# A fourth PSUM bank and another product order for layer 1, and a float64 conversion in 7 operations of 512 columns, in an attention, mixture and feed-forward kernel

## The chip, the cores and the metric

The kernel runs on one core of one Trainium2 chip, as one launch. The metric is the device time of one execution in microseconds (us). Before the change it is 1487.26 us, the median of three runs (1483.48 to 1487.72).

## The reference

Three blocks follow one another. Attention with a band of local keys and a few global keys (2 batches, 8 heads, 768 positions, 64 wide) gives x, 1536 tokens by 512. A mixture of 8 experts and a feed-forward layer then transform it:

```python
P = exp(x @ w_gate - max)
for _ in range(8):
    P /= P.sum(1) + 1e-9;  P /= P.sum(0) + 1e-9;  P *= N / E
for e in range(8):                       # w1[e]: 512 x 1024, w2[e]: 1024 x 512
    out += P[:, e:e+1] * (np.maximum(x @ w1[e], 0) @ w2[e])
h = out @ w_in                           # w_in: 512 x 2048
result = (h * (1 / (1 + np.exp(-1.702 * h)))) @ w_out
```

The last two matrices, w_in and w_out, reach the device as 64-bit floats; the rest is in 32 bits. The device therefore has to make 32-bit floats of w_in and w_out with integer operations before it can use them.

## The kernel before

**Units and steps.** Experts and the feed-forward layer are cut into units of 256 hidden columns: 32 units of the experts (four of each) and 8 of the feed-forward layer. A step works one unit on one of the two batches of 768 tokens, and there are 80 steps, laid out by `plan` (L531). A version is one loading of a unit's weights; most versions serve two steps in a row, one for each batch.

A step is a layer 1 (x by the unit's part of w1, `layer1`, L393) and a layer 2 (hidden values by the unit's part of w2, `layer2`, L472). On TensorE's queue layer 1 of step i stands ahead of layer 2 of step i-1, so layer 2 always reads hidden values that were finished a whole layer 2 earlier. Each full-precision product is made of three products of high and low parts (the names end in h and l, and the split is `split`, L196: ScalarE rounds the high part, GpSimd subtracts for the low part).

**Layer 1** multiplies a 2 by 2 block matrix by a 2 by 2 block matrix with seven products and not eight. Each product is 6 matmuls of 384 columns. The table PRODUCTS (L60) names, for each, the weight sum (A11, S2, ...), the operand sum (B11, T2, ...) and the PSUM bank that it accumulates in: x, y or z. Before, the order is A11 (x), S2 (y), A12 (x), S3 (y), S1 (z), A22 (y), S4 (z). Between the products VectorE forms the sums u2, u3 and p1 from the banks (the helper on L403), and ScalarE copies the first product to p1 (L452). A bank that goes on accumulating must first have been read by the sum that wants its value up to there. So S3 waits for the sum u2 that reads bank y after S2, with one product (A12) between the two; A22 waits for the sum u3 that reads y after S3, with one product (S1) between; S4 waits for the sum that reads z after S1, with one product (A22) between; A12 waits for the copy of x.

`put` (L408) takes a finished block of hidden values: ScalarE applies Relu or Sigmoid, and the rest (the low part, and in the feed-forward layer the multiplication with the sigmoid, L418) is queued behind the next product's matmuls (`late`). In the feed-forward layer each block needs one of two sigmoid buffers (tag "sg").

**Layer 2** has six tiles of 128 tokens, each of 6 matmuls of 512 columns, and each is read out of its PSUM bank by VectorE (L500 scaled by the gate, L498 and L506 without) or, for an expert's first unit, by ScalarE. `psum` (L519) hands out the banks: eight in all, two named s, two named t, one named v and three named m, which hold x, y and z. In phase 2 (attention of the second batch runs between the steps) layer 2 uses the m banks; in phase 3 (gate and normalisation run between the steps) it goes round s, s, t, v; in phase 4 (the rest) it goes round s, s, t, t, and bank v is idle.

**Work in between.** `mixture` (L600) calls `advance` after every product and every layer-2 tile, 13 times a step. Each call adds a rate to a debt, and for each whole number in the debt it emits the next piece of a side task, in the engines' queues at that place. From the step after the gate is ready, the side task is `doubles` (L221) at a rate of 0.55: it converts w_in and w_out and stores them in device memory for the feed-forward units, whose loads (`load_w1` and `load_w2`) come late in the plan. All loads and stores are issued from SyncE's queue.

`doubles` has 64 jobs of 256 columns. A job loads 256 KB (L239), makes nine VectorE operations of 128 by 256 in five pieces (L250 to L263), five with a constant and four with two tensors, all reading SBUF alone, and stores 128 KB (L264).

**Order on the engines.** All queues are in the order in which the program emits work, and VectorE, ScalarE and GpSimd each run theirs in order. Weight splits of the next version (`split_w1`, `split_w2`) are emitted in the second step of a version, one product behind the one that used the same buffer.

## Time and profile before

| what | value |
|---|---|
| median of three runs | 1487.26 us (1483.48 to 1487.72) |
| the profiled execution's own time | 1492.43 us |
| its span, first to last instruction | 1490.4 us |
| mean granted TensorE clock | 0.986 of full speed |
| TensorE matmul, busy | 1422.0 us, 95% |
| VectorE, busy | 1135.6 us, 76% |
| GpSimd, busy | 860.1 us, 58% |
| ScalarE, busy | 644.5 us, 43% |

The profile is of one execution, which took 5.2 us longer than the median of the runs; 2.0 us of its time lie outside the span. A busy engine in it is one with an instruction running; a matmul's end is modelled, so a short idle time of TensorE can be longer than its row says. PE is TensorE, PEld its weight loads, DVE VectorE, ACT ScalarE, POOL GpSimd and SP SyncE.

### The profile page before, as it was taken

What the parts mean: (1) busy time and instruction counts of PE and PEld (TensorE: products, weight loads), DVE (VectorE), ACT (ScalarE), POOL (GpSimd) and SP (SyncE); (2) the same over time, 40 slices, a digit from 0 to 9 for tenths busy, and PEclk for the clock granted to TensorE, in tenths of its full rate; (3) what the DMA queues carried; (4) which work ended last, traced back from release to release, by engine and by line L of the source; (5) the groups of instructions that cost most, each with busy time, mean ns of one, the idle gap of its engine ahead of it and who ended that gap; (6) DMA issues with size and microseconds to landing.
All of it is one profiled execution on the core that took longest, in us unless ns stands there. A gap on an engine that the chain in (4) does not pass through costs nothing.

```text
span 1490.4 us, 21158 instructions
## 1 busy us (share of the span) xinstructions
PE 1422.0 (95%) x7295; PEld 1244.4 (83%) x7295; DVE 1135.6 (76%) x2199; ACT 644.5 (43%) x1511; POOL 860.1 (58%) x1003
## 2 busy tenths in 40 slices
PE   7899998999899999999999999999999988999999
PEld 5567887788888888898888888888888877899897
DVE  7987887467578888888888888788887576555655
ACT  5676767243443333333333333333333456534332
POOL 3645555657674555554555545455555686756652
PEclk9989999999999999999999999999999999999999
DMA  5322210111221222222121212112121111101002
GB/s 147 73 61 60 73 46 29 57 57 57 75 88 62 66 73 72 71 64 68 60 75 64 82 60 72 60 61 75 61 85 47 48 38 34 52 29 43 29 1 85
DMA packets 99348, 91.66 MB, mean 61 GB/s; under 512 B 42912, under 2 KB 76704, under 8 KB 99232
## 3 DMA queue, kind: packets, MB, share of 16 engines
q1 hardware_dynamic: 99232, 90.22, 19.2%
q8 instruction: 60, 0.98, 0.3%
q14 instruction: 56, 0.46, 0.1%
HBM read 78.66 MB, written 11.53 MB: 61 GB/s over the span
## 4 chain that ended last, share of the span: by engine, by line
PE 80%; DVE 13%; issue 3%; ACT 3%; POOL 2%; POOLq 0%; DVEq 0%; ACTq 0%
PE pl L489 41%; PE pl1y L445 14%; PE pl1z L445 10%; PE pl1x L445 8%; PE pv L928 2%; DVE u L403 2%; PE s L850 1%; DVE acc L500 1%; PE pt L887 1%; DVE a L876 1%; POOL w2l L205 1%; DVE acc L285 1%; DVE a L863 1%; DVE al L908 1%; DVE hl L430 1%
## 5 line engine op out<-in xcount | busy, mean ns | idle before, releaser
L489 PE MATMUL pl<-w2h,hl 128*128 128x512 f32 x960 | 300.9, 394 | 6.9 <-DVE acc L500 4.3
L489 PE MATMUL pl<-w2l,hh 128*128 128x512 f32 x960 | 297.2, 391 | 0.0
L489 PE MATMUL pl<-w2h,hh 128*128 128x512 f32 x960 | 297.1, 391 | 0.0
L500 DVE SCALAR_TENSOR_TENSOR acc<-pl,pr,acc 128x512 f32<-128x512 f32 x312 | 230.2, 746 | 74.5 <-PE pl L489 71.9
L205 POOL TENSOR_TENSOR w2l<-r,w2h 128x512 fp32r<-128x512 f32 x100 | 131.5, 1336 | 196.7 <-ACT w2h L199 178.1
L489 PEld LDWEIGHTS pl<-w2l,hh 128*128 128x128 f32 x960 | 180.5, 188 | 39.3
L489 PEld LDWEIGHTS pl<-w2h,hh 128*128 128x128 f32 x960 | 180.4, 188 | 38.8
L489 PEld LDWEIGHTS pl<-w2h,hl 128*128 128x128 f32 x960 | 176.8, 188 | 39.8 <-DVE acc L500 5.7
L425 POOL TENSOR_TENSOR hl<-u,hh 128x384 fp32r<-128x384 f32 x100 | 105.8, 1058 | 135.1 <-ACT hh L422 134.5
L199 ACT ACTIVATE w2h<-r 128x512 fp32r<-128x512 f32 x98 | 56.6, 624 | 207.6 <-PE pl L489 174.3
L403 DVE TENSOR_TENSOR u<-p,pl1y 128x384 f32<-128x384 f32 x160 | 87.8, 549 | 64.7 <-PE pl1y L445 52.5
L452 ACT ACTIVATE p<-pl1x 128x384 f32<-128x384 f32 x80 | 39.2, 490 | 182.2 <-PE pl1x L445 167.6
L403 DVE TENSOR_TENSOR u<-u,pl1z 128x384 f32<-128x384 f32 x160 | 88.1, 551 | 36.2 <-PE pl1z L445 33.7
L421 ACT ACTIVATE u<-u 128x384 f32<-128x384 f32 x100 | 52.1, 521 | 123.6 <-DVE u L403 123.1
L205 POOL TENSOR_TENSOR hl<-sg,hh 128x384 fp32r<-128x384 f32 x64 | 66.0, 1031 | 58.1 <-ACT hh L199 56.7
L205 POOL TENSOR_TENSOR S3l<-s,S3h 128x256 fp32r<-128x256 f32 x50 | 40.5, 810 | 99.4 <-ACT S3h L199 99.2
L192 POOL TENSOR_TENSOR s<-r 128x256 f32<-128x256 f32 x100 | 78.2, 782 | 0.0
L506 DVE TENSOR_TENSOR acc<-pl,acc 128x512 f32<-128x512 f32 x84 | 54.3, 682 | 19.9 <-PE pl L489 19.8
L866 ACT ACTIVATE a<-a,m 128x288 f32<-128x288 f32 (+2 forms) x96 | 48.1, 502 | 43.0 <-DVE m L863 43.0
L445 PE MATMUL pl1y<-T3h,S3l 128*128 128x384 f32 x160 | 44.4, 358 | 23.0 <-DVE u L403 22.9
L427 ACT ACTIVATE hh<-pl1x 128x384 fp32r<-128x384 f32 x64 | 31.4, 491 | 79.5 <-PE pl1x L445 79.4
L205 POOL TENSOR_TENSOR A22l<-r,A22h 128x256 fp32r<-128x256 f32 x50 | 44.0, 880 | 22.6 <-ACT A22h L199 22.3
(259 smaller groups left out, 3489.6 us busy)
## 6 DMA issues: line engine op xcount, KB each, us to landing
r<-in_moe_w_dram SPq DMA_DIRECT2D x82, 512.0 KB, 3.6
r<-d SPq DMA_DIRECT2D x18, 512.0 KB, 3.7
d<-in_moe_w_in_dram SPq DMA_DIRECT2D x32, 256.0 KB, 2.8
d<-cx SPq DMA_DIRECT2D x64, 128.0 KB, 1.7
d<-in_moe_w_out_dram SPq DMA_DIRECT2D x32, 256.0 KB, 3.0
out_dram<-acc SPq DMA_DIRECT2D x12, 256.0 KB, 2.1
k<-in_k_dram SPq DMA_DIRECT2D x28, 96.0 KB, 2.3
q<-in_q_dram SPq DMA_DIRECT2D x28, 96.0 KB, 2.5
```

The source lines that it names most:

```text
L192: nc.gpsimd.tensor_tensor(out=o, in0=x, in1=y, op=op)
L199: nc.scalar.activation(hi, x, AF.Copy)
L205: e.tensor_tensor(out=lo, in0=x, in1=f(hi), op=ALU.subtract)
L403: add = lambda o, x, y: nc.vector.tensor_tensor(out=o, in0=x, in1=y, op=ALU.add)
L421: nc.scalar.activation(c, c, AF.Relu)
L425: nc.gpsimd.tensor_tensor(out=l, in0=c, in1=f(h), op=ALU.subtract)
L445: nc.tensor.matmul(ps, x[:, d, :], y[:, d, :], start=(new and i == 0 and d == 0), stop=(i == 2 and d == 1), skip_group_check=True)
L452: nc.scalar.activation(p1, ps, AF.Copy)
L489: nc.tensor.matmul(ps, x[:, c, ts_], y, start=(i == 0 and c == 0), stop=(i == 2 and c == 1))
L500: nc.vector.scalar_tensor_tensor(out=acc, in0=ps, scalar=self.pr[:, tt, e : e + 1], in1=acc, op0=ALU.mult, op1=ALU.add)
L506: nc.vector.tensor_tensor(out=acc, in0=ps, in1=acc, op=ALU.add)
L866: nc.scalar.activation(s, s, AF.Exp, bias=m, scale=-1.0, accum_out=rs[:, j : j + 1])
```

## The change

From phase 3 on, layer 1 uses another table, WIDE: S3 goes to a bank of its own (w, which is the bank named v), S3 and S1 come before A12, and A22 starts bank y anew and does not go on accumulating in it. The sums change with it: u3 = u2 + w after S3, p1 = u3 + z after S1 (and this block is put there), the block of x is put after A12, and u3 = u3 + y after A22. Every product, sum and put is still made once. In phase 3 layer 2 goes round s, s, t.

`doubles` has 32 jobs of 512 columns with seven operations (three with a constant, four with two tensors) in seven pieces, at a rate of 0.42. Loads are 512 KB each and stores 256 KB; there are 32 of each.

```diff
+    WIDE = [
+        ("A11", "B11", "x"),
+        ("S2", "T2", "y"),
+        ("S3", "T3", "w"),
+        ("S1", "T1", "z"),
+        ("A12", "B21", "x"),
         ("A22", "T4", "y"),
         ("S4", "B22", "z"),
     ]
...
-        C = 256
+        C = 2 * FW
...
-                for _ in range(8):
+                for _ in range(6):
                     yield
...
             nc.vector.tensor_scalar(x, hi, 3, 0x3FFFFFFF, op0=ALU.logical_shift_left, op1=ALU.bitwise_and)
-            nc.vector.tensor_scalar(y, hi, -0x40000000, None, op0=ALU.bitwise_and)
-            yield
-            nc.vector.tensor_tensor(out=x, in0=x, in1=y, op=ALU.bitwise_or)
+            yield
+            nc.vector.scalar_tensor_tensor(out=x, in0=hi, scalar=-0x40000000, in1=x, op0=ALU.bitwise_and, op1=ALU.bitwise_or)
+            yield
+
             nc.vector.tensor_scalar(y, x, -0x800000, None, op0=ALU.bitwise_and)
             yield
-            nc.vector.tensor_scalar(z, lo, 1, None, op0=ALU.logical_shift_right)
-            nc.vector.scalar_tensor_tensor(out=f(z), in0=z, scalar=2.0**-51, in1=f(y), op0=ALU.mult, op1=ALU.mult)
-            yield
-            nc.vector.tensor_tensor(out=f(x), in0=f(x), in1=f(z), op=ALU.add)
+            nc.vector.scalar_tensor_tensor(out=f(y), in0=lo.bitcast(U32), scalar=2.0**-52, in1=f(y), op0=ALU.mult, op1=ALU.mult)
+            yield
+            nc.vector.tensor_tensor(out=f(x), in0=f(x), in1=f(y), op=ALU.add)
+            yield
...
-        for an, bn, k in [self.PRODUCTS[n] for n in (0, 4, 2, 1, 3, 5, 6)] if first else self.PRODUCTS:
+        wide = self.phase >= 3
+        order = self.WIDE if wide else self.PRODUCTS
+
+        for an, bn, k in [order[n] for n in (0, 4, 2, 1, 3, 5, 6)] if first else order:
             ah, al = self.w1[v, an]
             bh, bl = self.xops[b][bn]
-            new = k not in bank
-            if new:
-                bank[k] = self.ps_m.tile([P, HS], F32, tag="m", name=f"pl1{k}_{v}_{b}")
+            new = k not in bank or wide and an == "A22"
+            if k not in bank:
+                p, tag = (self.ps_v, "v") if k == "w" else (self.ps_m, "m")
+                bank[k] = p.tile([P, HS], F32, tag=tag, name=f"pl1{k}_{v}_{b}")
...
+            elif an == "S4":
+                add(u2, u2, ps)
+                put(u2, 0, 1)
+            elif wide:
+                if an == "S3":
+                    add(u3, u2, ps)
+                elif an == "S1":
+                    add(p1, u3, ps)
+                    put(p1, 1, 1)
+                elif an == "A22":
+                    add(u3, u3, ps)
+                    put(u3, 1, 0)
...
-            kinds = {2: "m", 3: "sstv", 4: "sstt"}[self.phase]
+            kinds = {2: "m", 3: "sst", 4: "sstt"}[self.phase]
...
-                    side.append(("doubles", self.doubles(self.cv), 0.55))
+                    side.append(("doubles", self.doubles(self.cv), 0.42))
```

## Rows read from the trace of the kernel before

**Rows 1.** Part 1 of the page: busy time, share of the span, instructions.

```profile
PE 1422.0 (95%) x7295; PEld 1244.4 (83%) x7295; DVE 1135.6 (76%) x2199; ACT 644.5 (43%) x1511; POOL 860.1 (58%) x1003
```

**Rows 2.** Windows: length; PE, PEld, DVE, ACT, POOL busy (instructions); clock, DMA, GB/s.

```profile
387.89:1178.64 790.75, 771.22 (x3823) 688.72 (x3822) 652.89 (x1167) 286.46 (x633) 438.96 (x484) 1.00 0.21 68
1147.59:1178.64 31.05, 31.05 (x157) 28.12 (x156) 15.62 (x24) 11.31 (x25) 17.74 (x21) 1.00 0.12 34
1307.73:1462.90 155.17, 155.17 (x782) 140.52 (x780) 93.41 (x150) 63.13 (x136) 93.29 (x101) 1.00 0.07 24
1400.83:1408.14 7.31, 7.31 (x44) 7.30 (x42) 3.49 (x7) 4.41 (x11) 5.95 (x7) 1.00 0.22 74
```

**Rows 3.** Waits of TensorE from 388 to 1179 us: total, times, longest.

```profile
PE pl1y L445 <- DVE u L403: 18.0, 22, 2.4
```

**Rows 4.** Timeline of VectorE, GpSimd and TensorE in a layer 1 at 709 us.

```profile
709.88 2.59 POOL L205 TENSOR_TENSOR w2l<-r,w2h 128x512 fp32r<-128x512 f32 x2 [5.64 <-ACT w2h L199]
...
711.36 1.40 DVE L257 SCALAR_TENSOR_TENSOR cz<-cz,cy 128x256 f32<-128x256 int32 x1
...
712.00 0.51 PE L445 MATMUL pl1x<-B21h,A12h 128*128 128x384 f32 x2
...
712.68 0.54 DVE L403 TENSOR_TENSOR u<-p,pl1y 128x384 f32<-128x384 f32 x1
...
713.27 0.61 PE L445 MATMUL pl1y<-T3h,S3l 128*128 128x384 f32 x2 [0.76 <-DVE u L403]
```

**Rows 5.** Windows: 2.55 us just after the longest wait of rows 3.

```profile
941.24:943.79 2.55, 2.55 (x9) 2.55 (x9) 0.56 (x1) 0.00 (x0) 0.00 (x0) 0.50 0.47 154
```

**Rows 6.** Waits of TensorE from 250 to 388 us.

```profile
PE pl1y L445 <- DVE u L403: 5.6, 2, 3.2
...
PE pl1z L445 <- DVE u L403: 0.7, 1, 0.7
```

**Rows 7.** Waits of TensorE from 1179 to 1308 us.

```profile
PE pl L489 <- DVE acc L500: 4.3, 4, 3.2
...
PE pl1y L445 <- DVE u L403: 1.3, 1, 1.3
```

**Rows 8.** Groups of VectorE, 388 to 1146 us: dearest and cheapest conversion operation.

```profile
L257 DVE SCALAR_TENSOR_TENSOR cz<-cz,cy 128x256 f32<-128x256 int32 x64 | 42.7, 668 | 2.2
...
L256 DVE TENSOR_SCALAR cz<-d 128x256 int32<-128x256 int32 x64 | 28.2, 441 | 0.0
```

**Rows 9.** Instructions by line: duration in ns min/median/max; L250, L253, L390, L500.

```profile
L250 DVE TENSOR_SCALAR cx<-d x64: 275/289/1373, 423.0 to 1136.9; 128x256 int32<-128x256 int32 x64
...
L253 DVE TENSOR_TENSOR cx<-cx,cy x64: 407/419/1384, 426.0 to 1138.0; 128x256 int32<-128x256 int32 x64
...
L390 DVE SCALAR_TENSOR_TENSOR acc<-acc,pr,acc x6: 752/990/1764, 355.7 to 370.7; 128x512 f32<-128x512 f32 x6
...
L500 DVE SCALAR_TENSOR_TENSOR acc<-pl,pr,acc x312: 732/750/753, 398.9 to 1239.4; 128x512 f32<-128x512 f32 x156
```

**Rows 10.** Part 6 of the page: DMA issues, KB each, us to landing.

```profile
r<-d SPq DMA_DIRECT2D x18, 512.0 KB, 3.7
```

**Rows 11.** Timeline of a layer 1 and layer 2 of the feed-forward stage.

```profile
1408.14 0.63 PE L489 MATMUL pl<-w2h,hl 128*128 128x512 f32 x2
...
1408.64 0.53 ACT L415 ACTIVATE sg<-p 128x384 f32<-128x384 f32 x1
...
1410.72 0.52 ACT L415 ACTIVATE sg<-u 128x384 f32<-128x384 f32 x1
...
1412.15 2.47 DVE L506 TENSOR_TENSOR acc<-pl,acc 128x512 f32<-128x512 f32 x4
```

**Rows 12.** Timeline of a layer 2 in phase 3.

```profile
379.69 0.63 PE L489 MATMUL pl<-w2h,hl 128*128 128x512 f32 x2
...
382.67 2.04 DVE L498 TENSOR_TENSOR accx<-pl,accx 128x512 f32<-128x512 f32 x3
```

More of the change, by code (lines that the diff above doesn't have):

```diff
@@ L10 @@
 I32 = mybir.dt.int32
+U32 = mybir.dt.uint32
 AF = mybir.ActivationFunctionType
@@ L65 @@
         ("S1", "T1", "z"),
+        ("A22", "T4", "y"),
+        ("S4", "B22", "z"),
+    ]
+    WIDE = [
[4 more added lines that the diff above has]
+        ("A12", "B21", "x"),
         ("A22", "T4", "y"),
@@ L225, in doubles @@
         nc = self.nc
-        C = 256
+        C = 2 * FW
         jobs = []
         for s in range(len(self.f1)):
-            for c in range(self.DC):
-                jobs.append((self.w_in[c * P : c * P + P, s * 2 * FW : (s + 1) * 2 * FW], self.f1[s][c]))
+            for c in range(0, self.DC, 2):
+                w = self.w_in[c * P : (c + 2) * P, s * 2 * FW : (s + 1) * 2 * FW]
+                jobs.append((w.rearrange("(c p) n -> p c n", p=P), self.f1[s][c : c + 2].rearrange("c p n -> p c n"), 2))
             for c in range(FW // P):
-                for h in range(512 // C):
-                    r = s * FW + c * P
-                    jobs.append((self.w_out[r : r + P, h * 2 * C : (h + 1) * 2 * C], self.f2[s][c, :, h * C : (h + 1) * C]))
+                r = s * FW + c * P
+                jobs.append((self.w_out[r : r + P, :], self.f2[s][c], 1))
         ds = {}
@@ L238, in doubles @@
                 ds[j] = cv.tile([P, C, 2], I32, tag="d", bufs=2, name=f"d_{j}")
-                nc.sync.dma_start(ds[j].rearrange("p n t -> p (n t)"), jobs[j][0])
+                o = ds[j].rearrange("p n t -> p (n t)")
+                nc.sync.dma_start(o.rearrange("p (c n) -> p c n", c=2) if jobs[j][2] == 2 else o, jobs[j][0])
             if j == 0:
-                for _ in range(8):
+                for _ in range(6):
                     yield
@@ L263, in doubles @@
             nc.vector.scalar_tensor_tensor(out=f(x), in0=f(y), scalar=TINY, in1=f(x), op0=ALU.is_ge, op1=ALU.mult)
-            nc.sync.dma_start(jobs[j - 1][1], f(x))
+            o = f(x)
+            nc.sync.dma_start(jobs[j - 1][1], o.rearrange("p (c n) -> p c n", c=2) if jobs[j - 1][2] == 2 else o)
             yield
@@ L461, in layer1 @@
                 put(p1, 1, 0)
-            elif an == "S4":
-                add(u2, u2, ps)
-                put(u2, 0, 1)
-            if an in ("S1", "S3") and {"S1", "S3"} <= seen:
+            if not wide and an in ("S1", "S3") and {"S1", "S3"} <= seen:
                 add(u3, u3, bank["z"])
```

1 line of the change is left out of this document (removed).

## The prediction

> **What bounds the kernel now.** I read the page's first part first: TensorE is busy 95% of the span, VectorE 76%, GpSimd 58% [rows 1]. So TensorE sets the end, and what can be won is its idle and slowed time, stage by stage. The windows give that. A step is 7 products of 6 matmuls and 6 tiles of 6, 78 matmuls. The stretch from 1307.73 to 1462.90 us, the feed-forward layer, holds 10 steps (782 matmuls) in 155.17 us, with TensorE busy all the time: 15.52 us a step [rows 2]. Its layer 1 takes 7.31 us [rows 2], so 1.04 us a product, and layer 2 the other 8.21 us, 1.37 us a tile. The stretch from 387.89 to 1178.64, phase 4 up to the end of the plain expert steps, holds 49 steps (3823 matmuls) in 790.75 us, 16.14 us a step [rows 2]. 49 steps of 15.52 us would be 760.5 us. **This stage loses 30.3 us.**
>
> Who takes them is in the waits: 22 waits on the sums of L403, 18.0 us [rows 3], nearly all of them before bank y is accumulated further. The rest of the 30.3 us lies beside these rows. A stall costs more than its row, because the end of the matmul before is modelled: in the layer 1 at 709 us the row says 0.76 us, but from the start of the last pair of A12 to the first of S3 it is 1.27 us, where a pair takes 0.35 us, so 0.92 us were lost [rows 4]. After the longest wait, 2.4 us [rows 3], the granted clock is 0.50 for 2.55 us, the level of 1.2 GHz and not 2.4, so half of those 2.55 us went too [rows 5].
>
> Why is VectorE late? In rows 4 GpSimd runs two weight splits, 2.59 us, and a conversion operation that alone takes 0.42 us [its kind: rows 9] lasts 1.40 us beside them. Behind it in VectorE's queue stands the sum u2, which begins only at 712.68 and frees bank y at 713.22, while A12, the one product between, was over by 712.35. In the two steps after the conversion, 1147.59 to 1178.64, TensorE loses nothing (31.05 of 31.05 us), and VectorE is busy 15.62 us, 7.8 us a step; with the conversion it is 652.89 / 49 = 13.3 us a step [rows 2].
>
> **The change part by part.** *The fourth bank and the order.* No product, sum or put is added. The waits move. S3 writes bank w, last read in the step before, and S1 bank z: neither waits any more. A22 starts y anew and waits for u2, now with three products after S2 and not one: 3.12 us where it was 1.04. S4 waits for p1 = u3 + z with two products between, 2.08 us for 1.04. A12 waits for the copy of x with three products between, not one. In rows 4 u2 ends some 1.9 us after S2's matmuls (712.35 less 1.04 us is 711.31). That is under 3.12. The sums u3 and p1 follow it, 0.54 us each, and p1 ends near 714.3, with one conversion operation between still before 715.5, when S4 would begin (711.31 + 4 products). The longest wait, 2.4 us past a cover of 1.04, made u2 end 3.5 us after S2: 0.4 us would be left. So at most a few tenths stay in a few steps. What could stay is bounded by nothing and by half of 30.3; I take 2 us, near the low end because only one wait of rows 3 is known to pass the new cover. **Stage: -28.3 us.** What is behind S4's wait is its six matmuls and then all of layer 2, so that is where a late p1 would show.
>
> The same order holds in phase 3. Its waits on these sums are 5.6 us in two and 0.7 us [rows 6]: the 3.2 us one is within the new cover (1.04 + 3.2 = 4.2 us against 3.12 leaves 1.1 at the worst, and its u2 was late from work that ran beside A12). I count between nothing and 6.3 us and take 4.8. After 1179 us one wait of 1.3 us goes [rows 7]; the 4.3 us of waits for L500 there stand in layer 2 [rows 7] and stay. **-6.1 us.**
>
> *What the new order makes late.* The blocks to be put come after S1, A12, A22 and S4, four in a row, before after A12, S1, A22 and S4. In the feed-forward steps each block is a chain over ScalarE, VectorE and GpSimd: from one sigmoid to the next 2.08 us (1408.64 to 1410.72) [rows 11]. The chain starts one product earlier than the last three blocks did, and is one block longer, so it ends 2.08 - 1.04 = 1.0 us later, and layer 2's reading stands behind it in VectorE's queue. That reading now starts at 1412.15, its first tile is out at 1412.77 (a quarter of 2.47 us later), and the fifth tile, which needs the same bank, begins at 1408.14 + 4 x 1.37 = 1413.6 [rows 11]. Spare 0.8 us, so 0.2 us over. Sixteen feed-forward steps: 0 to 5 us (0.3 each); I take **+3 us**. In phase 3 layer 2 has three banks and not four: its first tile is read at 382.67 and out 0.68 us later (383.35), and the fourth begins at 379.69 + 4.1 = 383.8 [rows 12]; a chain later by one block of some 1.7 us would cost 1.2 us a step, in 7 steps 0 to 8.6 us. Evidence is thin, since most of these steps wait for little; I take **+2 us**.
>
> *The conversion.* It lies wholly on VectorE and SyncE's queue, so what it saves is only lateness, and I count it at nothing beyond the stage above. Its size matters for the cover, though. 576 operations now cost VectorE 652.89 - 49 x 7.81 = 270 us, 0.47 us each with overlaps [rows 2]; singly they take between 0.44 and 0.67 us [rows 8]. New are 224 operations. Undisturbed, 256 columns take 0.275 us with a constant and 0.407 with two tensors [rows 9], so columns cost 0.5 and 1.0 ns and 512 of them 0.41 and 0.67 us; a two-tensor operation of 512 columns in SBUF takes 0.75 [rows 9]. A job of three and four is then 3.9 us, and with the present wait per operation (270 / 64 = 4.2 us a job, less 3.0 undisturbed, over nine operations: 0.13 us) 4.8 us; 32 jobs are 154 us. If waits doubled with the columns it would be 7/9 of 270, 210 us. I take 154, because reading PSUM, where nothing contends, L500 stays at 732 to 753 ns, while L250 goes from 275 to 1373 [rows 9]: the excess has about the size of one GpSimd operation (2.59 / 2 us) [rows 4].
>
> The Trainium skill says the same of it as a rule: in "SBUF — State Buffer", section "SBUF: two separate sides", VectorE and GpSimd share one pair of ports as an exclusive lock held for a whole instruction. By that rule the wait does not grow with the columns of the waiting operation, and the sum would be the 154 us; by the rows alone it could be 210.
>
> Pieces: before 8 + 64 x 5 = 328 at 0.55, 596 calls or 45.9 steps of 13; after 6 + 32 x 7 = 230 at 0.42, 548 calls or 42.1 steps. So VectorE gets 154 / 42.1 = 3.7 us a step beside 7.8, 11.5 of 15.52 us (5.0 and 12.8 by the upper end), and the conversion is done four steps sooner, ahead of its loads. A piece is one operation and not mostly two, so a sum stands behind less. The DMAs are half as many and twice as large; 512 KB land in 3.7 us [rows 10], a job lasts 7 / 0.42 = 16.7 calls, some 20 us, and covers them. The stores wait in SyncE's queue as before, with weight loads behind them that are wanted a version later.
>
> **Sum:** -28.3 - 6.1 + 3 + 2 = -29.4 us. From the profiled execution's 1492.4 us that is 1463.0; that execution took 5.2 us longer than the median, so against the median 1487.26 - 29.4 = **1458 us**.
>
> **The rivals.** *Half of the waits move on.* VectorE is still late, and p1 comes too late for S4, or layer 2's reading does. For it: u2, u3 and p1 now stand closely one behind the other. Against: with 1.04 us of cover only 22 of 49 steps had such a wait [rows 3], and VectorE gets free time. The stage gives back 15.2 and not 28.3 us: 1471 us.
>
> *The change does not do what it says.* Bank w is no free bank in effect, or the wait for VectorE only changes its place, because one queue makes all sums: the waits come back whole, at A22, S4 and in layer 2. Then -1.3 + 5, some 1487 to 1491 us, no change that shows. Against it: the 3.12 us above.
>
> *VectorE becomes the bound.* The place is the conversion stage: 0.42 x 13 = 5.46 operations a step, and 15.52 - 7.8 = 7.7 us for them. From 1.41 us an operation VectorE sets the step; the time passes that of before at about 1.55 us. If integers of 32 bits without sign, read with a stride and multiplied as floats, were that slow, or each operation waited out a whole GpSimd operation of 1.3 us and then took 0.6, a step were 7.8 + 5.46 x 1.9 = 18.2 us, and 42 steps 112 us above 15.52 each: 1458 + 110 = 1568 us. Against: no kind of operation in rows 8 has a mean over 0.67 us, and twice that is 1.34.
>
> By the skill's rule just named such a wait is one GpSimd instruction at the most, and comes only where one is running; GpSimd's 17.74 of 31.05 us [rows 2] agree with neither extreme. The chance of this case is small by the rows and by the rule.
>
> **How the numbers follow.** Forecast 0.78, half 0.13, no gain 0.05, VectorE bound 0.04. The forecast's own range: at its low end nothing stays in the stage and nothing new comes, -30.3 - 6.3 - 1.3 = -37.9, 1449 us; at its high end the new waits cost 5 + 8.6 and the stage keeps 4, 1469 us. To hold 8 in 10 the range reaches to the half case: 1449 to 1472 us. A measurement of this kernel can tell about 0.3%, 4.5 us, from no change: faster 0.91 (forecast and half), same 0.05, slower 0.04.
>
> **What would show it.** Right: the window from the first phase 4 step over 49 steps is near 762 us, waits of bank y's matmuls on L403's sums are nearly gone, VectorE is busy some 11 to 12 us a step in the conversion, and there are 224 operations of 0.5 to 0.9 us that end some four steps sooner. Layer 2 in the feed-forward steps waits a few tenths for L506, where it now waits for nothing. Wrong: waits before bank z's second product (S4) or layer 2's first matmuls of several tenths in most steps, or conversion operations with a mean over 1.3 us.

## The result, and the profile after

The changed kernel takes **1463.38 us**, the median of four runs (1462.28 to 1464.26). The kernel before, run beside it on the same chip, takes 1487.49 us (1483.48 to 1489.29). The ratio is 0.9841, with a 95% interval of 0.982 to 0.9862: 24.1 us or 1.6% faster. The prediction was 1458 us with a range of 1449 to 1472. The profiled execution took 1463.75 us, its span is 1461.8 us.

Part 1 of the page of the changed kernel answers to [rows 1]:

```profile
PE 1409.9 (96%) x7295; PEld 1244.0 (85%) x7295; DVE 1005.5 (69%) x1847; ACT 642.1 (44%) x1511; POOL 870.7 (60%) x1003
```

TensorE makes the same 7295 matmuls. VectorE has 352 operations fewer and 130 us less to do.

The windows show where the time went. I cut both traces at the same steps: the first row is steps 6 to 12 (phase 3), the second the 49 plain expert steps of [rows 2], the third the last two of these, the fourth steps 62 to 67 (the last expert steps and the first feed-forward steps, where the normalised sums are turned into the operands of the feed-forward layer), the fifth the other feed-forward steps up to the start of the last one. Steps count from 0. The columns are those of [rows 2]. First the kernel after:

```profile
248.68:386.10 137.42, 126.93 (x619) 106.97 (x617) 88.78 (x179) 48.89 (x114) 90.43 (x103) 0.96 0.17 54
386.10:1146.11 760.01, 760.01 (x3823) 689.17 (x3822) 524.70 (x815) 286.06 (x633) 450.98 (x484) 1.00 0.21 71
1115.10:1146.11 31.01, 31.01 (x157) 28.13 (x156) 15.40 (x24) 11.24 (x25) 17.07 (x21) 1.00 0.11 35
1146.11:1263.18 117.07, 104.16 (x517) 90.57 (x516) 68.28 (x89) 64.07 (x132) 89.86 (x90) 0.97 0.13 41
1263.18:1433.89 170.71, 170.71 (x859) 154.66 (x858) 103.35 (x164) 68.59 (x148) 99.86 (x109) 1.00 0.08 25
```

Then the two stretches of the kernel before that [rows 2] don't have:

```profile
252.05:387.89 135.84, 126.06 (x618) 106.42 (x617) 89.17 (x179) 48.78 (x114) 90.79 (x103) 0.97 0.16 55
...
1178.64:1291.88 113.24, 102.73 (x518) 90.24 (x516) 71.02 (x89) 64.63 (x132) 89.56 (x90) 0.98 0.13 42
```

| stretch | before | after | difference | predicted |
|---|---|---|---|---|
| steps 6 to 12 | 135.84 | 137.42 | +1.6 | -2.8 |
| 49 plain expert steps | 790.75 | 760.01 | **-30.7** | -28.3 |
| steps 62 to 67 | 113.24 | 117.07 | +3.8 | -1.3 |
| feed-forward steps after that | 171.02 | 170.71 | -0.3 | +3 |

The predicted +3 is for sixteen feed-forward steps. Eleven of them are in the last row, four in the row above it, and the last one lies behind it.

The four differences sum to -25.6 us. The spans differ by 28.6: another 3.35 us are won ahead of the first layer 1 (98.52 before, 95.17 after), a part that the change does not touch and that lasted between 89.5 and 98.5 us in the kernels of this study, and 0.3 us are lost behind the start of the last step.

The stage of the 49 steps now loses nothing: TensorE is busy 760.01 of 760.01 us, 15.51 us a step, which is what the steps without the conversion take (31.01 us for two). No row of TensorE's waits is left in it, where [rows 3] had 22 waits. The waits of the kernel after in steps 6 to 12 and, in a second fence, in steps 62 to 67 (total us, times, longest; the sums' helper is now on L416, layer 1's matmuls on L462, layer 2's on L515, its readings on L524 to L532):

```profile
PE pl L515 <- DVE accx L524: 5.4, 3, 3.7
...
PE pl1z L462 <- DVE p L416: 2.0, 1, 2.0
```

```profile
PE pl L515 <- DVE acc L526: 4.5, 4, 2.1
PE pl L515 <- ACT acc L530: 4.1, 2, 3.6
PE pr L542 <- DVE acc L526: 3.0, 1, 3.0
PE pl1y L462 <- DVE u L416: 0.8, 1, 0.8
```

Against [rows 6] the 5.6 us for bank y are gone, and 5.4 us before layer 2 and 2.0 us before bank z have come. Two waits of 3 us and more stand in steps 62 to 67; the experiments come back to both stretches.

The conversion's operations, by line (ns min/median/max, first to last start), answer to [rows 9]:

```profile
L261 DVE TENSOR_SCALAR cx<-d x32: 416/490/1393, 421.1 to 1038.4; 128x512 int32<-128x512 int32 x32
...
L275 DVE SCALAR_TENSOR_TENSOR cx<-cy,cx x32: 682/686/1656, 437.7 to 1054.0; 128x512 f32<-128x512 f32 x32
```

Undisturbed they take 0.42 and 0.68 us. All 224 cost VectorE 524.70 - 49 x 7.70 = 147 us (7.70 is half of the third window's 15.40). The last one starts 668 us after the stage does, 43.1 of its steps in.

### The profile page after: what moved, and what is told of

It reads as the page before. It is cut to its first block, busy times and chain, and to the rows that moved or that the text cites. A ratio compares the mean times of both kernels' runs of the same rounds, so it can differ in the third digit from the quotient of the medians.

```text
span 1461.8 us, 20827 instructions
## 1 busy us (share of the span) xinstructions
PE 1409.9 (96%) x7295; PEld 1244.0 (85%) x7295; DVE 1005.5 (69%) x1847; ACT 642.1 (44%) x1511; POOL 870.7 (60%) x1003
## 4 chain that ended last, share of the span: by engine, by line
PE 70%; DVE 2%; ACT 1%; POOL 1%; issue 1%; DVEq 0%; ACTq 0%
PE pl L515 37%; PE pl1x L462 9%; PE pl1y L462 9%; PE pl1z L462 9%; PE pl1w L462 5%; DVE sg L431 1%; ACT sg L428 0%; DVE acc L526 0%; DVE acc L298 0%; PE pr L542 0%; ACT hh L210 0%; DVE p L416 0%; POOL s L203 0%; DVE u L416 0%; POOL hl L216 0%
## 5 line engine op out<-in xcount | busy, mean ns | idle before, releaser
L515 PE MATMUL pl<-w2h,hl 128*128 128x512 f32 x960 | 303.6, 398 | 14.2 <-DVE accx L524 5.4
L526 DVE SCALAR_TENSOR_TENSOR acc<-pl,pr,acc 128x512 f32<-128x512 f32 x312 | 233.2, 749 | 120.8 <-PE pl L515 118.9
L515 PE MATMUL pl<-w2l,hh 128*128 128x512 f32 x960 | 299.5, 393 | 1.0 <-POOL w2l L216 1.0
L515 PE MATMUL pl<-w2h,hh 128*128 128x512 f32 x960 | 298.8, 393 | 0.0
L515 PEld LDWEIGHTS pl<-w2h,hl 128*128 128x128 f32 x960 | 177.0, 189 | 49.1 <-DVE accx L524 6.6
L515 PEld LDWEIGHTS pl<-w2l,hh 128*128 128x128 f32 x960 | 181.7, 189 | 41.4 <-POOL w2l L216 1.9
L515 PEld LDWEIGHTS pl<-w2h,hh 128*128 128x128 f32 x960 | 181.5, 189 | 39.0
L210 ACT ACTIVATE w2h<-r 128x512 fp32r<-128x512 f32 x98 | 56.5, 624 | 201.6 <-PE pl L515 163.2
L438 POOL TENSOR_TENSOR hl<-p,hh 128x384 fp32r<-128x384 f32 x50 | 50.8, 1015 | 97.0 <-ACT hh L435 97.0
L416 DVE TENSOR_TENSOR u<-p,pl1y 128x384 f32<-128x384 f32 x86 | 47.5, 552 | 79.0 <-PE pl1y L462 67.6
L434 ACT ACTIVATE p<-p 128x384 f32<-128x384 f32 x50 | 26.3, 526 | 134.9 <-DVE p L416 134.9
L443 DVE SCALAR_TENSOR_TENSOR hl<-pl1x,hh 128x384 fp32r<-128x384 f32 x64 | 35.6, 557 | 66.7 <-ACT hh L440 66.3
L203 POOL TENSOR_TENSOR s<-r 128x256 f32<-128x256 f32 x100 | 78.8, 788 | 0.0
L532 DVE TENSOR_TENSOR acc<-pl,acc 128x512 f32<-128x512 f32 x84 | 54.2, 682 | 13.8 <-PE pl L515 12.7
```

What stands on the lines that cost most here:

```text
L203: nc.gpsimd.tensor_tensor(out=o, in0=x, in1=y, op=op)
L210: nc.scalar.activation(hi, x, AF.Copy)
L416: add = lambda o, x, y: nc.vector.tensor_tensor(out=o, in0=x, in1=y, op=ALU.add)
L434: nc.scalar.activation(c, c, AF.Relu)
L438: nc.gpsimd.tensor_tensor(out=l, in0=c, in1=f(h), op=ALU.subtract)
L515: nc.tensor.matmul(ps, x[:, c, ts_], y, start=(i == 0 and c == 0), stop=(i == 2 and c == 1))
```

## The experiments

The change has two parts that aim at the same waits, so the first question was which of them took the 30.7 us away. **My theory** was that of the prediction: the bank and the order give the late sum u2 three products of cover, and the shorter conversion is worth nothing beyond that. **The rival**: the conversion makes u2 less late, and that alone would do. A smaller theory was to be tested for each of the other three stretches. All ratios are to the kernel before, run on the same chip.

### 1. The bank and the order alone

The old conversion is kept; the rest is the change.

```diff
+        wide = self.phase >= 3
+        order = self.WIDE if wide else self.PRODUCTS
...
                     side.append(("doubles", self.doubles(self.cv), 0.55))
```

> The fourth bank and the new order alone; the conversion stays at nine operations on 256 columns in 64 jobs, rate 0.55. Theory (cover): the 30 us of the 49 plain expert steps were lost because one product (1.04 us) was too little time for a late sum, and the new order gives two to three. Then this stage takes 760 to 764 us as with the whole change (760.0), against 790.8 before, and the time is 1463 to 1468 us. Rival (shorter conversion): VectorE is late because of the conversion's operations, and only fewer of them make it punctual. Then the lateness turns up at S4 and in layer 2, the stage stays above 775 us and the time above 1478 us.

Measured: 1463.27 us (1461.01 to 1466.42), ratio 0.9831 (0.981 to 0.9853). Its window of the 49 steps, and in a second fence its waits there:

```profile
386.34:1150.46 764.12, 762.64 (x3823) 688.47 (x3822) 640.24 (x1167) 286.82 (x633) 439.73 (x484) 1.00 0.21 70
```

```profile
PE pl1z L460 <- DVE p L414: 1.0, 3, 0.6
...
PE pl1y L460 <- DVE u L414: 0.3, 1, 0.3
```

VectorE's work is close to that of before (640 us against 653), with the same 1167 operations. Still 26.6 of the 30.7 us are gone: what is left of the 22 waits is 1.3 us, most of it before S4 (pl1z), where the prediction had put what would stay. VectorE has not become punctual here: counted in the traces, u2 ends more than one product (1.04 us) after S2 in 36 of the 49 steps, where it did so in 22 before. So it is the cover that works.

### 2. The conversion alone

The diff of `doubles` and the rate 0.42, with the old products and banks.

```diff
-        C = 256
+        C = 2 * FW
...
-                    side.append(("doubles", self.doubles(self.cv), 0.55))
+                    side.append(("doubles", self.doubles(self.cv), 0.42))
```

> The conversion in seven operations on 512 columns alone; three banks and the order of before. Cover theory: a single operation beside a GpSimd split still lasts up to 1.4 to 1.7 us, longer than the one product of cover, so a good part of the waits stays: the 49 steps take 770 to 785 us and the time is 1467 to 1482 us. Rival (shorter conversion): the stage falls to 760 to 764 us, and since the stretches before and after it stay as they were, the time is 1456 to 1461 us, below the whole change.

Measured: 1458.43 us (1455.12 to 1460.67), ratio 0.9796 (0.9775 to 0.9818). The 49 steps take 762.66 us: 28.1 of the 30.7 us. Their window, and the only wait of TensorE in them:

```profile
383.60:1146.26 762.66, 761.66 (x3824) 688.55 (x3823) 533.66 (x815) 286.70 (x633) 450.93 (x484) 1.00 0.21 70
```

```profile
PE pl1x L448 <- ACT p L455: 0.9, 1, 0.9
```

**My expectation fell and the rival holds**: with one product of cover, as before, no wait on the sums is left in the stage; the one row is a wait for the copy of x. The timeline of a step with a weight split shows why (start us, length us, engine, line, operation; L406 is the sums' helper, L448 layer 1):

```profile
696.51 3.00 POOL L206 TENSOR_TENSOR w2l<-r,w2h 128x512 fp32r<-128x512 f32 x2 [5.74 <-ACT w2h L200]
...
696.69 1.66 DVE L265 SCALAR_TENSOR_TENSOR cx<-cy,cx 128x512 f32<-128x512 f32 x1
...
698.27 0.54 DVE L406 TENSOR_TENSOR u<-p,pl1y 128x384 f32<-128x384 f32 x1
...
698.97 0.51 PE L448 MATMUL pl1y<-T3h,S3l 128*128 128x384 f32 x2
```

As in [rows 4], a conversion operation runs beside GpSimd's weight splits and is held up, 1.66 us where it takes 0.68 alone. But it is the only one between layer 2's last reading and u2, and it had begun before S2's matmuls were over (698.97 - 1.04 = 697.93). So u2 ends at 698.81, 0.9 us after S2 and just inside A12. In [rows 4] it was 1.9 us after, because there a piece has two such operations; the timeline of VectorE in the kernel before has, just ahead of L257's row,

```profile
710.07 1.26 DVE L256 TENSOR_SCALAR cz<-d 128x256 int32<-128x256 int32 x1
```

Both are held up, 1.26 and 1.40 us. I had taken the 1.4 to 1.7 us of one held-up operation for longer than the cover of 1.04; what counts is the part of it that lies behind S2's end.

So each part alone takes nearly all of the waits away, and the two together only 2.7 and 4.1 us more than either. They are substitutes.

### 3. Bank without order

As in 1, but A12 keeps its place between S2 and S3: S3 has a bank of its own and the sums change as in WIDE.

```diff
         ("S2", "T2", "y"),
+        ("A12", "B21", "x"),
         ("S3", "T3", "w"),
         ("S1", "T1", "z"),
-        ("A12", "B21", "x"),
         ("A22", "T4", "y"),
```

> The fourth bank alone: S3 in bank w, A22 starting y anew and the sums of the change, but the products in the order of before (A12 third) and the conversion of before. In the run with the order the sum u2 ended as late as before (1.9 us after S2's matmuls in most of the steps with a weight split), and the stage still fell to 764.1 us. Theory (the bank does it): S3's wait was the one that cost, and behind it the sums catch up while PE goes on, so that S4 with one product of cover waits little. Then the 49 steps take 762 to 767 us, and since the block of x is put early as before, steps 62 to 67 take 113 to 114.5 us; the time is 1460 to 1466 us. Rival (the order is needed): p1 comes too late for S4 by 0.5 us and more in some 20 steps, the stage takes 772 us or more, the time 1470 us or more.

Measured: 1477.97 us (1476.09 to 1481.79), ratio 0.9944 (0.9925 to 0.9963); the 49 steps take 782.02 us, only 8.7 less than before. The window and the waits of that stage:

```profile
380.69:1162.71 782.02, 767.19 (x3823) 687.99 (x3822) 655.77 (x1167) 286.43 (x633) 437.82 (x484) 1.00 0.21 69
```

```profile
PE pl1z L460 <- DVE p L414: 13.3, 22, 1.5
```

The 22 waits before bank y of [rows 3] are now 22 waits before bank z. In this order S4 starts one product (A22) after S1 instead of two, and p1 hangs on u2 by way of u3. The free bank moves the wait from S3 to S4; the order is what gives S4 its cover. The rival of this experiment, that the order is needed, holds.

### 4. Shorter, or fewer at once?

In experiment 2 the conversion is shorter (147 instead of 270 us) and also comes one operation at a time instead of mostly two. Experiment 2's conversion with two operations in most pieces, at the rate for as many pieces:

```diff
             nc.vector.tensor_scalar(x, hi, 3, 0x3FFFFFFF, op0=ALU.logical_shift_left, op1=ALU.bitwise_and)
-            yield
             nc.vector.scalar_tensor_tensor(out=x, in0=hi, scalar=-0x40000000, in1=x, op0=ALU.bitwise_and, op1=ALU.bitwise_or)
             yield
...
-                    side.append(("doubles", self.doubles(self.cv), 0.42))
+                    side.append(("doubles", self.doubles(self.cv), 0.24))
```

> The conversion alone, with the same seven operations on 512 columns and as many steps, but emitted two at a time (rate 0.24 for 0.42), on the banks and the order of before. VectorE's total work is that of the conversion run, whose 49 steps took 762.7 us with nearly no waits. Theory (the lump): what made u2 late was two conversion operations in front of it, each held up by a GpSimd split; one is done within the time of A12. Then pairs bring the waits back in those steps where a pair falls there, about every second one with a weight split: the stage takes 768 to 780 us, the time 1464 to 1476 us. Rival (the load): VectorE is punctual because it has 2 us a step more of free time; the stage stays at 762 to 765 us and the time at 1456 to 1461 us.

Measured: 1477.76 us (1476.82 to 1479.59), ratio 0.9936 (0.9913 to 0.996). VectorE's busy time in the 49 steps is about that of experiment 2, 547.0 and 533.7 us, but they take 780.85 us instead of 762.66, a little more than I had expected, and the waits on the sums are back:

```profile
382.79:1163.64 780.85, 767.41 (x3823) 687.83 (x3822) 547.02 (x815) 287.09 (x633) 447.83 (x484) 1.00 0.20 69
```

```profile
PE pl1y L445 <- DVE u L403: 10.5, 15, 1.2
...
PE pl1z L445 <- DVE u L403: 1.6, 5, 0.6
```

The converse is the old conversion, nine operations of 256 columns, each a piece of its own:

```diff
             nc.vector.tensor_scalar(x, hi, 3, 0x3FFFFFFF, op0=ALU.logical_shift_left, op1=ALU.bitwise_and)
+            yield
             nc.vector.tensor_scalar(y, hi, -0x40000000, None, op0=ALU.bitwise_and)
...
-                    side.append(("doubles", self.doubles(self.cv), 0.55))
+                    side.append(("doubles", self.doubles(self.cv), 0.99))
```

> The kernel before with its nine operations on 256 columns emitted one to a piece and not mostly two, at rate 0.99, so that the conversion takes as many steps. Theory (operations ahead of u2): between the last tile of layer 2 and u2 there are two calls, so two operations again stand ahead of u2 beside the weight split, as with 0.55 pieces of nearly two; the stage stays at 783 to 793 us and the time at 1480 to 1491 us. Rival (the size of a piece): single operations never lump, the stage falls to 762 to 770 us and the time to 1459 to 1467 us.

Measured: 1482.88 us (1479.93 to 1487.83), ratio 0.9969 (0.9948 to 0.999); the 49 steps take 785.47 us. Its window and its waits in them:

```profile
387.81:1173.28 785.47, 768.75 (x3823) 687.34 (x3822) 642.38 (x1167) 286.74 (x633) 438.07 (x484) 1.00 0.21 68
```

```profile
PE pl1y L448 <- DVE u L406: 15.8, 22, 0.9
```

Again 22 waits, but none over 0.9 us where [rows 3] had 2.4. At a rate of 0.99 a piece is emitted after nearly every product and tile, at 0.42 after four in ten, so nearly every u2 has operations of the conversion ahead of it. The pairs show that VectorE's total does not decide (nor the fewer and larger transfers, which they share with experiment 2), the nine single ones that issuing them singly is not enough.

The theory that the operations in the queue ahead of u2 decide can be counted in the traces. For each of the 49 steps I count the conversion operations that VectorE runs between its last reading of layer 2 and u2, and call u2 late when it ends more than 1.04 us after S2's matmuls:

| kernel, old banks and order | steps with two or more ahead | of them late | steps with one or none | of them late |
|---|---|---|---|---|
| before | 38 | 21 | 11 | 1 |
| experiment 2 | 1 | 0 | 48 | 2 |
| new, pairs | 16 | 8 | 33 | 1 |
| old, nine pieces | 44 | 22 | 5 | 1 |

With two or more ahead u2 is late in 51 of 99 steps, with one or none in 5 of 97. In the late ones the operations ahead take 2.7 to 3.1 us together (the medians of before, the pairs and the nine pieces), in the others 0.7 to 1.4. So in nearly all cases it takes two or more of them, held up; the new conversion brings their number down in both ways, by fewer operations and by one to a piece.

### 5. Twice the conversion, with the cover and without

If the two parts are substitutes, the bank and the order should be worth much more where the conversion is heavier. A job of the new conversion has 14 operations instead of seven (those that may be repeated without another result are made two or three times), at a rate of 0.84; in the whole change, and in the kernel of experiment 2.

```diff
             nc.vector.tensor_scalar(x, hi, 3, 0x3FFFFFFF, op0=ALU.logical_shift_left, op1=ALU.bitwise_and)
             yield
+            nc.vector.tensor_scalar(x, hi, 3, 0x3FFFFFFF, op0=ALU.logical_shift_left, op1=ALU.bitwise_and)
+            yield
...
-                    side.append(("doubles", self.doubles(self.cv), 0.42))
+                    side.append(("doubles", self.doubles(self.cv), 0.84))
```

> The whole change with the conversion's work doubled: each job runs 14 operations and not 7 (those that can be repeated without another result are run twice or three times), one to a piece, at rate 0.84, so as many steps as before. VectorE's work in the 49 steps was 10.7 us a step with the whole change, 3.0 of it the conversion; it becomes about 14.7 of 15.5 us. Theory (the order and the bank give cover): TensorE still does not wait much, 762 to 772 us in the stage, 1465 to 1476 us in all. Rival (VectorE becomes the bound): its backlog grows into layer 2 and S4, the stage takes 785 us or more, 1488 us or more.

> The same doubled conversion without the fourth bank and on the order of before. With 0.84 operations a call, one or two conversion operations stand ahead of u2 in every step, as in the kernel before. Theory (two ways to one end): the waits are back, the stage takes 785 to 805 us and the time is 1481 to 1502 us, 15 to 35 us above the same work on the new order; that is what the bank and the order are worth. Rival (the lump alone matters, single pieces suffice): 762 to 770 us in the stage, 1458 to 1466 us.

Measured: with bank and order 1470.47 us (1467.54 to 1471.13), ratio 0.9882 (0.9864 to 0.99); without 1508.12 us (1505.96 to 1508.95), ratio 1.0136 (1.0119 to 1.0153). The 49 steps with them, and their waits:

```profile
386.83:1156.04 769.21, 766.04 (x3823) 688.00 (x3822) 668.81 (x1039) 287.34 (x633) 487.70 (x484) 1.00 0.21 70
```

```profile
PE pl1z L474 <- DVE p L428: 2.6, 8, 0.6
```

and without:

```profile
384.61:1192.76 808.15, 777.37 (x3824) 688.53 (x3822) 690.80 (x1039) 286.81 (x633) 486.24 (x484) 1.00 0.20 66
```

```profile
PE pl1y L460 <- DVE u L418: 29.2, 38, 2.4
```

VectorE has about the same to do in both, and more than in the kernel before. Without the cover there are 38 waits and the stage loses 48 us, 3 more than the top of my expectation; with the cover it loses 9. Counted as in experiment 4, without the cover two or more operations stand ahead of u2 in 29 steps and it is late in 26 of them; of the 20 steps with fewer it is late in 6. Under this load the bank and the order are worth 37.7 us; beside the change's own light conversion they win 2.7 us in the stage and nothing over the whole kernel: by the medians the conversion alone is 5 us faster than the whole change (experiment 2), and from the first layer 1 to the end the two profiles agree to 0.6 us. The windows of the 49 steps side by side (us; 760.0 is no loss):

| conversion | three banks, old order | bank, old order | bank and order |
|---|---|---|---|
| old (9 x 256, five pieces) | 790.8 (before) | 782.0 | 764.1 |
| old, nine pieces | 785.5 | | |
| new, pairs | 780.9 | | |
| new (7 x 512) | 762.7 | 761.2 (experiment 7) | 760.0 (after) |
| new, doubled | 808.2 | | 769.2 |

### 6. Phase 3 with four banks for layer 2

The change gives bank v to layer 1 and leaves layer 2 three banks in phase 3. Here it goes round s, s, t, t.

```diff
-            kinds = {2: "m", 3: "sst", 4: "sstt"}[self.phase]
+            kinds = {2: "m", 3: "sstt", 4: "sstt"}[self.phase]
```

> The whole change, but in phase 3 layer 2 goes round s, s, t, t, four banks, and not s, s, t. Theory (three banks): layer 2 of the last step but one of phase 3 lost 7.0 us (15.2 for 8.2) because VectorE stood 3 to 5 us behind the combining of two experts' sums and the fourth tile wants the first one's bank; with four banks the cover is one tile (1.37 us) more at each of its two waits, so steps 6 to 12 fall from 137.4 to 132 to 135 us and the time to 1458 to 1461 us. Rival: the lateness is longer than a bank can cover, or the t banks are held by the gate's transposes: 137 us or more, 1463 us or more.

Measured: 1460.2 us (1457.8 to 1463.73), ratio 0.9822 (0.9798 to 0.9846); steps 6 to 12:

```profile
247.11:381.79 134.68, 124.35 (x619) 104.08 (x618) 89.43 (x179) 48.87 (x114) 91.04 (x103) 1.00 0.17 55
```

That is 2.7 us less than after, and the granted clock is 1.00 and not 0.96. The largest difference is in one place, the layer 2 that follows layer 1 of step 11: 15.23 us after, 9.85 here. About half of these 5.4 us is lost again: layer 1 of step 12 takes 1.1 us more here than after, and the layer 2 that follow the layer 1 of steps 7 to 9 together 2.0 us more. The timeline of the changed kernel at the large one (in its numbering L403 is VectorE combining two expert sums, L401 its GpSimd half, L203 the weight sums of a later version):

```profile
362.24 1.18 POOL L203 TENSOR_TENSOR s<-r 128x256 f32<-128x256 f32 x1
...
365.57 0.69 POOL L401 TENSOR_SCALAR acc<-acc,pr 128x512 f32<-128x512 f32 x1
...
366.29 0.75 DVE L403 SCALAR_TENSOR_TENSOR acc<-acc,pr,acc 128x512 f32<-128x512 f32 x1 [2.86 <-POOL acc L401]
366.96 1.88 DVE L524 TENSOR_TENSOR accx<-pl,accx 128x512 f32<-128x512 f32 x3
...
367.70 1.22 PE L515 MATMUL pl<-w2h,hl 128*128 128x512 f32 x2 [3.71 <-DVE accx L524]
```

VectorE's combining waits 2.86 us for GpSimd, which makes weight sums first; the readings of layer 2 stand behind it, three tiles at once, and with three banks TensorE waits 3.71 us. The 2.72 us after that wait run at half clock, the level of 1.2 GHz:

```profile
367.70:370.42 2.72, 2.72 (x6) 2.15 (x7) 1.14 (x2) 0.14 (x1) 0.00 (x0) 0.50 0.00 0
```

### 7. Four banks in phase 3 with the other parts varied

Two combinations looked for a version better than the whole change. One has experiment 6's line and lets the feed-forward steps use the old order; the other has experiment 6's line and experiment 3's order.

```diff
-        wide = self.phase >= 3
+        wide = self.phase >= 3 and not ffn
...
-            kinds = {2: "m", 3: "sst", 4: "sstt"}[self.phase]
+            kinds = {2: "m", 3: "sstt", 4: "sstt"}[self.phase]
```

> The whole change with both mended: four banks for layer 2 in phase 3, and the order and banks of before in the feed-forward steps. If the two losses are separate, steps 6 to 12 take 134 to 135.5 us, the 49 steps 760, steps 62 to 67 113.5 to 115: the time is 1454 to 1458 us, 5 to 9 us below the whole change and no more than level with the conversion alone or 4 us below it. Rival: they only move lateness from one place to another, 1459 us or more.

> The whole change, but the products in the order of before (A12 third, with S3 in bank w) and four banks for layer 2 in phase 3. If the order only matters for S4's cover, and the conversion has made VectorE punctual, then the 49 steps take 760 to 761.5 us, steps 6 to 12 take 133 to 136 us, and steps 62 to 67 113 to 115 us because the blocks are put as before: 1453 to 1457 us. Rival: with one product of cover S4 waits in the late steps of phase 3 and beside the second operands, 1459 us or more.

Measured: 1456.46 us (1456.27 to 1464.82), ratio 0.9806 (0.978 to 0.9832), with 135.0, 759.8 and 115.0 us in the first, second and fourth stretch; and 1457.37 us (1454.27 to 1462.89), ratio 0.9801 (0.9776 to 0.9826), with 136.7 (a little above the expectation), 761.2 and 114.3. The four banks bring steps 6 to 12 to 135 us a second time where the order is kept (137.6 without them, in experiment 8, the same kernel but for this line). Together with experiment 2 these are the three fastest, within 2 us of one another and not to be told apart; by the medians they are 5 to 7 us faster than the change as it was made. Not all of that is the edits': their profiled spans are 3.0 to 7.3 us shorter, and only 0.6 to 2.9 us of it lie behind the start of the first layer 1; the rest lies ahead of it, in the part that none of these kernels changes. With the light conversion, bank without order loses only 1.2 us of the stage.

### 8. The old order in the feed-forward steps

```diff
-        wide = self.phase >= 3
+        wide = self.phase >= 3 and not ffn
```

> The whole change, but the 16 feed-forward steps keep the three banks and the order of before. Theory (later chain): the stretch of steps 62 to 67, where experts and feed-forward alternate and the second batch's operands are made, went from 113.2 to 117.1 us because four blocks put in a row hold VectorE longer ahead of layer 2's reading. Then it falls to 113 to 114.5 us, the waits of 0.02 to 0.07 us in a few of the last steps go too, and the time is 1459 to 1461 us. Rival: the loss is of the operands' own work, which only lies otherwise in time: the stretch stays at 116 us or more, and waits on bank y come back beside it, 1463 to 1466 us.

Measured: 1461.78 us (1461.03 to 1462.35), ratio 0.9828 (0.9811 to 0.9844). Steps 62 to 67 take 114.91 us, between the two expectations, so the window alone settles nothing. The waits tell more. Here TensorE waits for ScalarE's reading (L530) and before the transposition into the feed-forward operands (L542) for

```profile
PE pl L515 <- ACT acc L530: 2.5, 1, 2.5
...
PE pr L542 <- DVE acc L526: 1.3, 1, 1.3
```

against 4.1 (longest 3.6) and 3.0 us in the changed kernel. The first of the two divides the kernels: a longest wait of 3.6 us in all four with the new order in the feed-forward steps (after, experiments 1 and 6, and experiment 5 with the cover), 2.5 in eight of the nine without (experiment 5 without the cover has 4.4). The second does so less clearly: 2.6 to 3.1 us in the four, 1.0 to 1.4 in eight of the others, 3.1 in one. The timeline of the changed kernel at the first of them (hh L210 is the last block's high part; L530 reads layer 2 out of its banks, because this step begins a new sum):

```profile
1222.91 0.52 ACT L428 ACTIVATE sg<-u 128x384 f32<-128x384 f32 x1
...
1224.44 0.52 ACT L210 ACTIVATE hh<-sg 128x384 fp32r<-128x384 f32 x1 [0.27 <-DVE sg L431]
1224.87 2.04 ACT L530 ACTIVATE acc<-pl 128x512 f32<-128x512 f32 x4
1225.50 1.22 PE L515 MATMUL pl<-w2h,hl 128*128 128x512 f32 x2 [3.59 <-ACT acc L530]
1226.52 1.06 PE L515 MATMUL pl<-w2l,hh 128*128 128x512 f32 x2
```

ScalarE, whose queue runs in order, reads four tiles only after the chain of sigmoids, 8.61 us after layer 2 began. The first kernel of experiment 7 has the old order here. The beginnings of this layer 2, first in the changed kernel, then in that one, and its ScalarE reading:

```profile
1216.26 0.63 PE L515 MATMUL pl<-w2h,hl 128*128 128x512 f32 x2
```

```profile
1210.68 0.63 PE L515 MATMUL pl<-w2h,hl 128*128 128x512 f32 x2
...
1218.22 2.04 ACT L530 ACTIVATE acc<-pl 128x512 f32<-128x512 f32 x4
```

There it is 7.54 us, 1.07 us earlier. That is the prediction's chain, later by one block's 1.0 us, but in front of ScalarE's reading and mainly in one step, not in front of VectorE's in sixteen. Over the whole stretch the four kernels of the new order take 117.1, 114.7, 116.3 and 112.5 us, in the mean 115.1; the nine of the old order in these steps 112.8 to 115.0, in the mean 114.0. By the means 1.2 us of the 3.8 are of the order, by the two pairs of rows 3.6 (1.6 and 2.0 more than before). How much it is stays open; for the scatter the last section has a cause.

## Why the prediction was right, and where it was not

**The stage, -28.3 us: measured -30.7.** TensorE was the bound and its idle time there was what could be won (30.3 predicted, 30.7 measured). The mechanism was shown by experiment 1: nothing but bank and order, 26.6 us, with u2 late in more steps than before. The 2 us that the term left in the stage are there in experiment 1 (4.1 us; of the 1.3 us that its rows show, 1.0 stand before S4, as said); beside the new conversion they are nothing.

**The conversion, "at nothing beyond the stage above": this step failed.** The term adds nothing to the sum, because the stage can't give back more than it loses, and so the number came out right. But the sentence behind it, that the conversion's part would only be lateness to be covered, hid that it removes that lateness: alone it wins 28.1 us, more than bank and order. The prediction had the sentence for it ("a sum stands behind less") and didn't work it out. On the layer 1 of [rows 4] it would have been: two held-up operations from 710.07 on let u2 end at 713.22; one of 1.66 us (as in experiment 2) would let it end near 710.07 + 1.66 + 0.54 = 712.27, 0.96 us after S2's end at 711.31 and inside A12's 1.04.

**The conversion's own price: right.** 0.42 and 0.68 us undisturbed (0.41 and 0.67 predicted), 147 us in all (154), done 43.1 steps into the stage (42.1). The open choice was whether a wait beside GpSimd grows with the columns. It does not: by line, the longest operation is 0.97 to 1.10 us over the shortest on 256 columns (L250: 275 to 1373 ns) and 0.97 to 1.02 us on 512 (L275: 682 to 1656); in the mean an operation takes 0.23 us more than the shortest of its line before, and 0.20 after. The Trainium skill has a rule for it in "SBUF — State Buffer", section "SBUF: two separate sides": the pair of ports that VectorE and GpSimd share is an exclusive lock, held for a whole instruction. By that rule a wait is at most one instruction of the other engine, whatever the columns of the one that waits. These rows agree: all the excesses are below the 1.3 us of one weight split in [rows 4].

**Phase 3, -4.8 + 2 for steps 6 to 12: measured +1.6.** The +2 for three banks was near: 2.7 us by experiment 6. The -4.8 failed. The waits of [rows 6] went, as said, but with four banks the stretch is only 1.2 us shorter than before. The trace of experiment 6 has its waits in other places: 2.0 us before S4, the rest before layer 2 and the gate's work. From layer 1 to layer 1 its seven layer 1 take 6.6 us less than before, and the seven layer 2 behind them 5.4 us more: here the waits did move on. That was the first rival, right for these seven steps and wrong for the 49.

**Feed-forward, +3: measured -0.3 in the eleven steps of the last row.** The chain's end is indeed later, but VectorE's reading starts 11.89 us after a step's first product (and 11.74 in every second step) where it was 11.32 (1412.15 - 1400.83) [rows 2, 11] (and 11.27): 0.5 to 0.6 us later and not 1.0, and the spare 0.8 us covers that. A step of the changed kernel, its first matmul and that reading:

```profile
1371.83 0.51 PE L462 MATMUL pl1x<-B11h,A11l 128*128 128x384 f32 x2
...
1383.72 3.18 DVE L532 TENSOR_TENSOR acc<-pl,acc 128x512 f32<-128x512 f32 x5
```

The block of x, now in the chain, needs no sum of its own; that the chain is shorter for this reason was not tested. The cost came at a reading that I had not looked at, ScalarE's in the first feed-forward step (experiment 8).

**After 1179, -1.3: measured +3.8** in the profiled execution; experiment 8 puts part of it on the order, at ScalarE's reading in a feed-forward step, and how large a part stays open.

**The sum.** -29.4 was predicted; the profiled executions differ by 28.7 us, the medians by 24.1. Errors of both signs met: the stage gave 2.4 us more, the other three stretches together 6.2 less (+5.1 where -1.1 was predicted). Subtracting from the median a sum made on an execution 5.2 us above it gave 1458; the sum itself gave 1463.0, and the profiled execution took 1463.75. That this agrees so well is luck: 3.35 us of the difference lie ahead of the first layer 1, where nothing was changed.

**The rivals.** VectorE as the bound is out: the dearest kind of operation has a mean of 0.91 us, where it would have taken 1.41. No gain is out, by the interval.

## What to carry to other kernels

Where a product accumulates in a bank that another engine must read first, count two things: the products between (the cover), and the operations that can stand in the reader's queue ahead of it, and how long each lasts when another engine holds it up. More cover and a shorter queue are substitutes, so their gains don't add: here 26.6 and 28.1 us alone, 30.7 together, and the cover is worth 37.7 where the queue is long. An extra bank is paid for where it is taken away, and whatever ends later in a new order is to be followed to every engine that reads behind it, also in the one step that reads in another way.

## What I had not expected of the hardware

A wait of the same length, at the same place, is followed by half clock in one execution and by full clock in another. After the wait of 3.59 us for L530 the changed kernel is granted 0.50 (the level of 1.2 GHz and not 2.4), its six pairs of matmuls from 1225.50 to 1230.78 take 5.28 us; in experiment 5 with the cover a wait of 3.57 us at the same instruction is followed by 1.00, and the six pairs take 2.86 us (1233.34 to 1236.20). The windows of 4 us behind the wait, first of the changed kernel, then of that run:

```profile
1225.50:1229.50 4.00, 4.00 (x9) 3.14 (x10) 4.00 (x4) 3.29 (x6) 2.26 (x2) 0.50 0.00 0
```

```profile
1233.34:1237.34 4.00, 4.00 (x19) 3.50 (x20) 3.37 (x3) 4.00 (x8) 0.64 (x1) 1.00 0.00 0
```

Experiments 1 and 6 have the 3.59 us and full clock as well, while among the kernels with 2.5 us there some show half clock and some don't. That is 2.4 us of the 4.6 by which steps 62 to 67 differ between these two kernels, and why a stretch with few waits of this size can't be told apart by a single profile. What decides between the two was not tried.
